# A fused attention, expert and gated-MLP kernel: the gate's tables behind group seven, one block of queries a group later, and unit 2's weights split in the units' loop

## The chip, the cores and the metric

The kernel runs on one core of a Trainium2 chip. The metric is the device time of one execution in microseconds (us); the time before is a median of three runs. The engines are named as the profile names them: PE (TensorE, matmuls; PEld its weight loads), DVE (VectorE), ACT (ScalarE), POOL (GpSimd) and SP (SyncE, which here only issues transfers).

## The reference

Three parts follow one another, on 2 x 768 tokens:

```python
# 1 attention, 2 batches x 8 heads, 768 tokens, head size 64
k_sum = k.reshape(B, H, nb, 32, D).max(axis=3)      # block maxima of the keys
v_sum = v.reshape(B, H, nb, 32, D).mean(axis=3)     # block means of the values
scores = [local scores (|i-j| < 16, else -1e9), scores with k_sum + log(32)]
a = softmax(scores); x = a @ [v, v_sum]             # then [1536, 512]
# 2 eight experts, each token goes to one
logits = x @ w_gate + modality_bias[modality_id]
e = argmax(logits); x = softmax(logits)[e] * (relu(x @ w1[e]) @ w2[e])
# 3 a dense layer 512 -> 2048 -> 512
h = x @ w_in; out = (h * tanh(softplus(h))) @ w_out
```

## The kernel before

**Attention.** It runs in 24 groups: 128 queries of one batch and of four heads each. A loop over steps g works on several groups at once: in step g it issues the scores of group g + 2 (`scores`), their row maxima on DVE (`top`, tile `nm`), the exponentials on ACT (`exps`, tile `a`), the reciprocal of their sums on DVE (tile `sm`) and the product of both (`normalize`, tile `an`, on DVE or POOL by the string `norm_by`), then the transposes of group g (`transpose_a`, `store_aT`) and the product with the values of group g - 1 (`values`, `store_xT`). All instructions of one engine run in the order in which this code issues them; semaphores order the engines among each other.

**What feeds the groups.** The tables `loads` and `prep`, by step, say when blocks of 256 queries or keys are loaded (SP) and prepared. A block is copied to `hp` (`pack`, one step ahead, engine by the fifth entry), transposed on PE, and written to SBUF: keys to `kt` (then, one step later, block maxima `ks` on DVE and windows `kw` on DVE or ACT), queries to `qb` in two halves (`q_chunk`, engines by the last entry: "VV" is both halves on DVE, "AV" the first on ACT, the second on DVE). A block is written ("q", batch, half of the heads, third of the tokens). POOL also adds up the values' block means (`vb`, `vm`), which come by transfer.

**The gate.** `small_loads` fetches three small inputs (`gm`, `mb`, `mi`) and `gate_tables` makes two tables of them on POOL: the identity beside the gate's weights in `gm`, which the first `gate_products` reads in step 10, and `bias_t`, which the first `choose` reads in step 12.

**Experts and dense layer.** Behind the groups stand 40 units of the experts' work (`step(u)`: `up_unit`, then `expert_down`, 24 and 12 matmuls on PE). Each needs its two weight tiles split into a high and a low part: `split_unit` issues one copy on ACT (`h`, L417) and one subtraction on DVE (`l`, L418) for each half. The table `hooks` starts this work inside the last groups: the splits of units 0, 1 and 2 in steps 22 and 24 and the first matmuls of unit 0 in step 25. In `step(u)` stands, for each unit, `split_unit(u + 1, 0)`, `split_unit(u, 1)`, `split_unit(u + 1, 1)`, `split_unit(u + 2, 0)`; a half that is split already is passed over. The accumulators of `expert_down` lie where the attention's PSUM tiles (`px` among them) lay. The dense layer is the last part.

Of the kernel before, what the change touches and what calls it, by code (L numbers as in the profile page):

```python
# [119 lines left out]
def attention_moe_mish_kernel(  # L120
# [17 lines left out]
    V, A, G, T = nc.vector, nc.scalar, nc.gpsimd, nc.tensor  # L138
# [282 lines left out]
    def load_w1(e, f, r1):  # L421
        nc.sync.dma_start(out=r1, in_=w1v[bass.ds(e, 1), :, :, f * 128:(f + 1) * 128].rearrange("o p k f -> p (o k) f"))

    def load_w2(e, f, r2):
        nc.sync.dma_start(out=r2, in_=w2v[bass.ds(e, 1), :, f, :].rearrange("o p d -> p (o d)"))
# [176 lines left out]
    def expert_reg(s):  # L602

        if s == 1:
            e_regs[1] = e_regs[0]
            return
        e = tab[0:1, 0, 0:1] if s == 3 else e_early[0:1, 0:1] if s == 0 else tab[0:1, 0, NSLOT:]
        e_regs[s] = reg(e, [ET.SP], E - 1)
# [9 lines left out]
    def load_first(n):  # L618

        for u in heads[:n + 1]:  # L620
            s, f = units[u]
            if (u, 0) not in asked and s in e_regs:
                asked.add((u, 0))
                raws[u, 0] = (extra if u == 3 else rw).tile([128, 4, 128], F32, tag="r1", name="r1")
                load_w1(e_regs[s], f, raws[u, 0])

    def load_second(u):
        if u >= len(units) or (u, 1) in asked or units[u][0] not in e_regs:
            return
        asked.add((u, 1))  # L630
        s, f = units[u]
        if s:
            raws[u, 1] = cout[:, NF2 // 2 + f, :].bitcast(F32)
        else:
            raws[u, 1] = extra.tile([128, DM], F32, tag="r2", name="r2", bufs=4)
        load_w2(e_regs[s], f, raws[u, 1])
# [377 lines left out]
    with ExitStack() as at:  # L1014
# [16 lines left out]
        raw, packed, kt, kw, ks, vw, vb, vm, qt = {}, {}, {}, {}, {}, {}, {}, {}, {}  # L1031
# [174 lines left out]
        def normalize(g, eng):  # L1206
            a, sm = st.pop(("a", g))
            an = thr.tile([128, 4, KC], F32, tag="an", name="an")
            eng.tensor_tensor(out=an, in0=a, in1=sm.unsqueeze(2).to_broadcast([128, 4, KC]), op=ALU.mult)
            st["an", g] = an  # L1210
# [177 lines left out]
        def gate_tables(mb, mi):  # L1388
            for j in range(4):
                G.tensor_scalar(out=gm[:, j, 0:128], in0=ident, scalar1=1.0, scalar2=0.0, op0=ALU.mult, op1=ALU.add)  # L1390
            mf = one.tile([128, 2, NT], F32, name="mf")
            mt = one.tile([128, 2, NT, E], F32, name="mt")
            for m in range(2):
                G.tensor_scalar(out=mf[:, m], in0=mi[:, :, 0], scalar1=float(m), scalar2=None, op0=ALU.is_equal)
                G.tensor_tensor(
                    out=mt[:, m], in0=mf[:, m].unsqueeze(2).to_broadcast([128, NT, E]),
                    in1=mb[:, m].unsqueeze(1).to_broadcast([128, NT, E]), op=ALU.mult,
                )
            G.tensor_tensor(out=bias_t, in0=mt[:, 0], in1=mt[:, 1], op=ALU.add)
# [48 lines left out]
            (22, 1): [("load",)],  # L1448
            (22, 2): [("split", 0), ("x", 1), ("x", 2), ("x", 3)],
            (24, 0): [("split", 1)],  # L1450
            (24, 2): [("split", 2)],
            (25, 0): [("up", 0)],
        }
        batches = [(0, 2), (2, 2), (4, 2), (6, 2), (8, 2)]
# [2 lines left out]
        def after(i, n):  # L1457
            return step_of[i] + n
# [88 lines left out]
        sums(1)  # L1547
        normalize(1, V)
        mb_mi = small_loads()
        gate_tables(*mb_mi)  # L1550

        def mixed(*parts):
            parts = list(parts)
# [7 lines left out]
        def mix(*parts):  # L1561
            for _ in mixed(*parts):
                pass
# [29 lines left out]
        def do_hook(x):  # L1593
            kind = x[0]
            if kind == "count":
                pc = pid[:, 448:448 + E]
                T.matmul(pc, cb[:, M_ONE:M_ONE + 128], ohsum)
                mix(choose_early(pc))
            elif kind == "load":
                expert_reg(0)  # L1600
                load_first(2)
                for u in range(3):
                    load_second(u)
            elif kind == "gather":
                V.tensor_copy(out=slot_ids, in_=pid[:, 0:E * NKP])
                of = small([128, NPIECE, E], "of")
                ids_ = pid[:, 0:E * NKP].rearrange("p (e k) -> p k e", e=E)[:, 0:NPIECE, :]
                V.tensor_tensor(out=of, in0=ids_, in1=early.unsqueeze(1).to_broadcast([128, NPIECE, E]), op=ALU.mult)
                fl = small([128, NPIECE], "fl")
                V.tensor_reduce(out=fl, in_=of, axis=AX.X, op=ALU.add)  # L1610
                V.tensor_copy(out=ids_early, in_=fl)
                xgs[0] = gather(None, new_rows())
                own()
                ids_reg(1)
            elif kind == "split":
                split_unit(x[1], 0)
                split_unit(x[1], 1)
                load_first(x[1] + 3)
                load_second(x[1] + 3)
            elif kind == "ids":  # L1620
                add_ids(*x[1:])
            elif kind == "x":
                some_x(0, x[1])
            elif kind == "up":
                up_unit(x[1])


        for g in range(NG + 2):
            if g == 16:
                first_p.close()  # L1630
                split_p = ctx.enter_context(tc.tile_pool(name="split", bufs=2, side="right"))
                cv = ctx.enter_context(tc.tile_pool(name="cv", bufs=1, side="right"))
                moe = ExitStack()
                late_moe = ExitStack()
                rw = ctx.enter_context(tc.tile_pool(name="rw", bufs=3, side="right"))
                hp = ctx.enter_context(tc.tile_pool(name="hp", bufs=2, side="right"))
                xp = ctx.enter_context(tc.tile_pool(name="xp", bufs=1, side="right"))
                extra = moe.enter_context(tc.tile_pool(name="extra", bufs=1, side="right"))
            for x in loads.get(g + 1, ()):
                do_load(x)  # L1640
            packs(g + 1)
            if g + 2 < NG:
                scores(g + 2)
                top(g + 2)
            for x in prep.get(g - 1, ()):
                if x[0] not in "qk":
                    do_prep(x)
            for i0, n in batches:
                if after(i0 + n - 1, 3) == g < NG and i0 != NEARLY:
                    add_ids(i0, n)  # L1650
            for x in hooks.get((g, 0), ()):
                do_hook(x)
            for x in prep.get(g, ()):
                if x[0] in "qk":
                    do_prep(x)
            if g < NG:
                if early_values[g]:
                    values(g - 1)
                transpose_a(g)
                if early_exps[g]:  # L1660
                    exps(g + 2)
                store_aT(g)
            if g + 2 < NG and not early_exps[g]:
                exps(g + 2)
            if g + 2 < NG - 1 or g == NG - 2:
                mix(place(g))
            for x in hooks.get((g, 1), ()):
                do_hook(x)
            if g + 2 < NG:
                sums(g + 2)  # L1670
                normalize(g + 2, V if norm_by[g + 2] == "V" else G)
            if g + 2 == NG - 1:
                mix(place(g))
            if 1 <= g <= NG:
                if g == NG or not early_values[g]:
                    values(g - 1)
                store_xT(g - 1)
            if g in gate_at:
                gate_products(gate_at[g])
                gate_store(gate_at[g])  # L1680
            for i0, n in batches:
                if step_of[i0 + n - 1] == g:
                    mix(choose(i0, n))
            if step_of[NT - 2] == g:
                mix(choose(NT - 2, 1))
            if step_of[NT - 2] + 1 == g:
                gate_exp(NT - 2, 1)
                mix(store_x(NT - 2, 1))
            if g in means_at:
                store_means(*means_at[g])  # L1690
            for x in hooks.get((g, 2), ()):
                do_hook(x)
# [122 lines left out]
```

## Time and profile before

| what | us |
|---|---|
| median of 3 runs (lowest, highest) | 572.18 (570.66, 573.83) |
| the profiled execution | 573.32 |
| its span | 571.3 |
| PE busy in the span | 533.4 |
| DVE, ACT, POOL busy | 390.7, 387.2, 95.5 |

The span is what the profile shows; 2.0 us lie around it. PE is busy for 93% of the span, but the first stages, up to some 140 us, are not bound by PE alone: there its waits are to be read one by one.

### The profile page before, as it was taken

Reading aid. Unit: us, or ns where it says so; the run is one execution under the profiler, and the core shown is the slowest. Engines: PE = TensorE matmul, PEld = TensorE weight load, DVE = VectorE, ACT = ScalarE, POOL = GpSimd, SP = SyncE. Lnnn points to the kernel's source line nnn. Section 1 sums busy time; section 2 is a strip of 40 time slices with the busy share of each in tenths; the row PEclk is TensorE's granted clock in tenths of the full one; section 3 lists DMA queues with packets and bytes.
Section 4 is the critical chain, followed back from the end, with each engine's and each line's share of the span. In section 5 each row is a group of like instructions: output and inputs, shape, how many; then the busy total and the mean of one; then the engine's idle time right before and its main releaser. Section 6 shows DMA issues by size and latency. Waiting matters only on the chain.

```text
span 571.3 us, 9001 instructions
## 1 busy us (share of the span) xinstructions
PE 533.4 (93%) x3086; PEld 462.7 (81%) x3086; DVE 390.7 (68%) x905; ACT 387.2 (68%) x793; POOL 95.5 (17%) x138
## 2 busy tenths in 40 slices
PE   4868799978999999999999999999999999999995
PEld 3857798868979998899988888888888888888883
DVE  3686889877777767688879998645664466456442
ACT  4756867566554535465578999778877887887771
POOL 5485542240604100000000000004000002100003
PEclk9998899989999999999999999999999999999999
DMA  8999961265754967634332331001000000100001
GB/s 210 176 226 205 181 107 37 75 170 183 242 178 142 335 198 244 211 121 129 111 112 80 104 107 41 1 1 73 1 0 1 0 2 37 38 0 1 0 1 73
DMA packets 75888, 59.34 MB, mean 104 GB/s; under 512 B 28838, under 2 KB 66214, under 8 KB 75456
## 3 DMA queue, kind: packets, MB, share of 16 engines
q1 hardware_dynamic: 73200, 52.36, 34.3%
q0 software_dynamic: 2640, 6.38, 3.2%
q8 instruction: 25, 0.41, 0.3%
q14 instruction: 23, 0.19, 0.1%
HBM read 51.25 MB, written 6.29 MB: 101 GB/s over the span
## 4 chain that ended last, share of the span: by engine, by line
PE 51%; DVE 2%; ACT 2%; issue 1%; POOL 0%; POOLq 0%; DVEq 0%
PE ph L539 22%; PE o L1719 22%; PE ph L467 4%; PE o L485 3%; ACT L577 0%; DVE l L418 0%; DVE cin L520 0%; DVE xg L580 0%; POOL out_dram L1736 0%; DVE mol L491 0%; ACT cin L516 0%; ACT xg L571 0%; ACT xg L577 0%; POOLq L1811 0%; DVE cin L519 0%
## 5 line engine op out<-in xcount | busy, mean ns | idle before, releaser
L580 DVE TENSOR_TENSOR xg<-xg,ph 128x512 f32<-128x512 f32 x48 | 30.8, 684 | 94.5 <-ACT xg L577 94.5
L571 ACT ACTIVATE xg<-ph,cf 128x512 f32<-128x512 f32 x48 | 33.0, 688 | 38.7 <-PE ph L539 38.0
L1736 POOL DMA_INDIRECT out_dram<-ot,rows x9 | 10.8, 1204 | 245.6 <-DVE xh L561 87.2
L467 PE MATMUL ph<-xh,h 128*128 128x290 f32 x160 | 50.2, 313 | 0.3 <-issue 0.3
L467 PE MATMUL ph<-xl,h 128*128 128x290 f32 x160 | 47.6, 297 | 0.4 <-DVE xl L451 0.4
L467 PE MATMUL ph<-xh,l 128*128 128x290 f32 x160 | 47.6, 298 | 0.3 <-DVE l L418 0.3
L1195 ACT ACTIVATE a<-ps,nm 128x120 f32<-128x120 f32 x96 | 33.4, 362 | 18.6 <-DVE nm L1187 12.1
L1181 PE MATMUL ps<-kw,qb 128*128 128x120 f32 x192 | 41.1, 342 | 5.1 <-DVE qb L1124 3.1
L1181 PEld LDWEIGHTS ps<-kw,qb 128*128 128x128 f32 x192 | 34.8, 227 | 7.7 <-ACT xT L1249 2.2
L539 PE MATMUL ph<-moh,l 128*128 128x512 f32 x96 | 38.0, 396 | 0.0
L1719 PE MATMUL o<-h,gl 128*128 128x512 f32 x96 | 37.9, 395 | 0.0
L1719 PE MATMUL o<-h,gh 128*128 128x512 f32 x96 | 37.9, 395 | 0.0
L1719 PE MATMUL o<-l,gh 128*128 128x512 f32 x96 | 37.9, 395 | 0.0
L539 PE MATMUL ph<-mol,h 128*128 128x512 f32 x96 | 37.9, 395 | 0.0
L539 PE MATMUL ph<-moh,h 128*128 128x512 f32 x96 | 37.9, 394 | 0.0
L417 ACT CAST h<-cout 128x512 fp32r<-128x512 f32 x32 | 19.8, 620 | 20.9 <-PE o L485 15.0
L539 PE MATMUL ph<-moh,xh 128*128 128x512 f32 x96 | 31.9, 393 | 0.0
L539 PE MATMUL ph<-moh,xl 128*128 128x512 f32 x96 | 31.9, 393 | 0.0
L467 PEld LDWEIGHTS ph<-xh,h 128*128 128x128 f32 x160 | 30.4, 190 | 1.4 <-issue 1.0
L467 PEld LDWEIGHTS ph<-xl,h 128*128 128x128 f32 x160 | 30.4, 190 | 1.3 <-issue 0.7
L572 ACT ACTIVATE xg<-xg 128x512 f32<-128x512 f32 x48 | 30.4, 632 | 1.5
L577 ACT ACT_TABLE_LOAD x24 | 30.8, 1283 | 0.4
(333 smaller groups left out, 1605.4 us busy)
## 6 DMA issues: line engine op xcount, KB each, us to landing
r<-in_moe_w_dram SPq DMA_DIRECT2D x32, 256.0 KB
cr<-in_moe_w_in_dram SPq DMA_DIRECT2D x16, 512.0 KB
cr<-in_moe_w_out_dram SPq DMA_DIRECT2D x16, 512.0 KB
cout<-in_moe_w_dram SPq DMA_DIRECT2D x16, 256.0 KB
cin<-in_moe_w_dram SPq DMA_DIRECT2D x16, 256.0 KB
k<-in_k_dram SPq DMA_DIRECT2D x12, 256.0 KB
q<-in_q_dram SPq DMA_DIRECT2D x12, 256.0 KB
vb<-in_v_dram SPq DMA_DIRECT2D x4, 768.0 KB
```

Source lines behind the costliest of these rows:

```text
L417: A.copy(out=h, in_=r)
L467: T.matmul(ph[:, :W], a[:, kk, :], b[:, kk, :], start=n == 0, stop=n == 11)
L485: T.matmul(po[d][:, :W], a[:, d * 128:(d + 1) * 128], b, start=f == 0 and n == 0, stop=f == F // 128 - 1 and n == 2)
L539: ins.append(T.matmul(pt, a[:, kk, :], b[:, kk, c0:c0 + 512], start=n == 0, stop=n == 11))
L571: A.activation(out=t, in_=hps, func=AF.Sigmoid, bias=cf[:, C_B0:C_B0 + 1])
L572: A.activation(out=t, in_=t, func=AF.Arctan)
L577: A.activation(out=t, in_=t, func=AF.Sin, scale=2.0)
L580: V.tensor_tensor(out=t, in0=t, in1=ph.pop(u), op=ALU.mult)
L1181: T.matmul(o, qc[:, j, t % 4, :], kw[b, hh][:, j, t, :], start=False, stop=True)
L1195: A.activation(out=a[:, j], in_=ps[:, j, 0:KC], func=AF.Exp, bias=nm[:, j:j + 1], accum_out=sm[:, j:j + 1],)
L1719: T.matmul(acc[m], a[:, m * 128:(m + 1) * 128], b, start=f == 0 and n == 0, stop=f == NF2 - 1 and n == 2)
L1736: ins = G.indirect_dma_start(out=out[:, :], out_offset=bass.IndirectOffsetOnAxis(ap=at_rows, axis=0), in_=ot[:, :], in_offset=None,)
```

## The change

The call of `gate_tables` moves from the place ahead of the loop to step 7 of the loop, behind that step's `normalize`. The block of queries ("q", 1, 1, 0) is prepared in step 10 instead of 9 (and so packed in step 9 instead of 8), and the first half of ("q", 1, 0, 0) is written by ACT instead of DVE. In step 24 unit 2 is no longer split; only the loads that came with it are issued there, and its two splits are issued by `step(0)` and `step(1)`.

```diff
-            9: [("kw", 1, 1, 1, "A"), ("kw", 1, 1, 2, "V"), ("k", 1, 1, 2, "G", "A"), ("q", 1, 0, 0, "G", "VV"), ("q", 1, 1, 0, "A", "VV")],
-            10: [("m2", 1, 1)],
+            9: [("kw", 1, 1, 1, "A"), ("kw", 1, 1, 2, "V"), ("k", 1, 1, 2, "G", "A"), ("q", 1, 0, 0, "G", "AV")],
+            10: [("q", 1, 1, 0, "A", "VV"), ("m2", 1, 1)],
...
-            (24, 2): [("split", 2)],
+            (24, 2): [("ahead", 5)],
...
         mb_mi = small_loads()
-        gate_tables(*mb_mi)
...
+            elif kind == "ahead":
+                load_first(x[1])
+                load_second(x[1])
...
                 normalize(g + 2, V if norm_by[g + 2] == "V" else G)
+            if g == 7:
+                gate_tables(*mb_mi)
```

On POOL the tables' six rows now stand behind the `normalize` of group 9 and ahead of the packing of the last block of keys and of the block of queries ("q", 1, 0, 0):

```order
 L1079 MEMSET kt 128x2x16
 L1209 TENSOR_TENSOR an<-a,sm 128x480
+L1390 TENSOR_SCALAR gm<-cf 128x128 x4
+L1394 TENSOR_SCALAR mf<-mi 128x12
+L1395 TENSOR_TENSOR mt<-mf,mb 128x96
+L1394 TENSOR_SCALAR mf<-mi 128x12
+L1395 TENSOR_TENSOR mt<-mf,mb 128x96
+L1399 TENSOR_TENSOR bias_t<-mt 128x96
 L1037 TENSOR_SCALAR hp<-k 128x512
 L1037 TENSOR_SCALAR hp<-q 128x512
```

The same six rows are gone from behind the first means (`vm`) and ahead of the `normalize` of group 2, where only two small memsets are left between the two.

On DVE, in steps 9 and 10, the rows of before read as follows (`qb_117` is the block ("q", 1, 0, 0), `qb_118` the block ("q", 1, 1, 0)):

```order
 L1187 TENSOR_REDUCE nm<-ps 128x4
 L1097 TENSOR_REDUCE ks<-kt 128x2x8 x2
-L1124 TENSOR_SCALAR qb_117<-ps 64x2x8x32 x2
-L1124 TENSOR_SCALAR qb_118<-ps 64x2x8x32 x2
+L1124 TENSOR_SCALAR qb_117<-ps 64x2x8x32
 L1203 TENSOR_SCALAR sm<-sm 128x4
 L1204 RECIPROCAL sm<-sm 128x4
```

Three of the four rows are gone there: one half of `qb_117` has moved to ACT, ahead of the exponentials of group 11, and DVE's own half waits for ACT's; the two of `qb_118` now stand one step later, behind the windows and ahead of the sums of group 12.

On ACT, where the units begin (`r_1712` and `r_1718` are unit 2's weight halves, `r_1735` one of unit 3's; `hh` is the hidden tile of units 0 and 1, `xr` copied from `px` frees the accumulators' place):

```order
 L1376 ACTIVATE xr<-xr,gs 128x512
+L473 ACTIVATE hh<-ph 128x290
+L1260 COPY xr<-px 128x512
 L417 CAST h<-r_1712 128x512
-L417 CAST h<-r_1718 128x512
-L473 ACTIVATE hh<-ph 128x290
-L1260 COPY xr<-px 128x512
 L1376 ACTIVATE xr<-xr,gs 128x512 x2
 L473 ACTIVATE hh<-ph 128x290
 L1289 ACTIVATE el<-lb 128x8
 L1376 ACTIVATE xr<-xr,gs 128x512
+L417 CAST h<-r_1718 128x512
```

Both casts stood ahead of the first `hh`; now one stands behind the copy of `px` and one behind the last scaling. DVE's two subtractions move in the same way. SP issues the same transfers in the same order as before.

## Rows read from the trace of the kernel before

**Rows 1.** Windows of the span: engines' busy time, PE clock, DMA share, GB/s

```profile
0.00:76.00 76.00, 56.57 (x379) 51.82 (x380) 53.83 (x100) 47.65 (x160) 44.76 (x69) 0.91 1.02 201
139.50:303.00 163.50, 160.75 (x1122) 149.02 (x1123) 124.72 (x318) 87.24 (x180) 18.93 (x28) 1.00 0.58 181
```

**Rows 2.** POOL's timeline, 18 to 37 us: start, duration, instruction, idle before and releaser

```profile
18.59 1.10 POOL L1390 TENSOR_SCALAR gm<-cf 128x128 f32<-128x128 f32 x4
27.50 0.26 POOL L1394 TENSOR_SCALAR mf<-mi 128x12 f32<-128x12 int32 x1 [7.81 <-DMA mi<-in_moe_modality_id_dram]
...
29.37 2.25 POOL L1209 TENSOR_TENSOR an<-a,sm 128x480 f32<-128x480 f32 x2
...
33.61 0.62 POOL L1037 TENSOR_SCALAR hp<-k 128x512 f32<-128x512 f32 x1 [1.20 <-DMA k<-in_k_dram]
34.20 2.35 POOL L1155 TENSOR_TENSOR vb<-vb 96x1024 f32<-96x1024 f32 x1
```

**Rows 3.** PE's timeline, 30 to 75 us, where it waited or a step begins

```profile
30.42 0.65 PE L1216 MATMUL pa<-cf,an 128*120 128x128 f32 x4 [1.78 <-POOL an L1209]
...
34.29 0.66 PE L1064 MATMUL px<-cf,hp 128*128 128x128 f32 x4 [0.58 <-POOL hp L1037]
...
38.37 0.45 PE L1181 MATMUL ps<-kw,qb 128*128 128x120 f32 x2 [2.04 <-DVE kw L1108]
...
68.57 0.74 PE L1181 MATMUL ps<-kw,qb 128*128 128x120 f32 x2
...
74.86 0.43 PE L1181 MATMUL ps<-kw,qb 128*128 128x120 f32 x2
```

**Rows 4.** DVE's timeline, 25 to 76 us

```profile
25.64 0.18 DVE L1204 RECIPROCAL sm<-sm 128x4 f32<-128x4 f32 x1
...
34.54 2.53 DVE L1103 COPY kw<-kt 128x960 f32<-128x960 f32 x1
...
49.71 2.75 DVE L1209 TENSOR_TENSOR an<-a,sm 128x480 f32<-128x480 f32 x1
...
62.88 2.32 DVE L1203 TENSOR_SCALAR sm<-sm 128x4 f32<-128x4 f32 x1
...
67.06 2.81 DVE L1124 TENSOR_SCALAR qb<-ps 64x512 f32<-64x512 f32 x4
...
72.98 0.65 DVE L1103 COPY kw<-kt 128x960 f32<-128x960 f32 x1
73.55 0.87 DVE L1108 COPY kw<-ks 128x576 f32<-128x576 f32 x1
74.35 1.23 DVE L1203 TENSOR_SCALAR sm<-sm 128x4 f32<-128x4 f32 x1
```

**Rows 5.** POOL's timeline, 49 to 75 us

```profile
49.58 5.39 POOL L1155 TENSOR_TENSOR vb<-vb 96x1024 f32<-96x1024 f32 x4 [3.37 <-DMA vb<-in_v_dram]
...
60.15 0.99 POOL L1209 TENSOR_TENSOR an<-a,sm 128x480 f32<-128x480 f32 x1 [2.10 <-ACT xT L1249]
61.10 0.96 POOL L1037 TENSOR_SCALAR hp<-k 128x512 f32<-128x512 f32 x1
...
62.61 2.56 POOL L1155 TENSOR_TENSOR vb<-vb 96x1024 f32<-96x1024 f32 x1
...
72.96 1.15 POOL L1037 TENSOR_SCALAR hp<-q 128x512 f32<-128x512 f32 x1 [1.46 <-DMA q<-in_q_dram]
```

**Rows 6.** Window of step 10, the same columns as rows 1

```profile
67.00:74.30 7.30, 5.80 (x28) 5.66 (x29) 6.23 (x12) 6.93 (x25) 2.33 (x3) 0.53 1.19 228
```

**Rows 7.** Timelines where the units begin: two rows of ACT, one of DVE, one of PE

```profile
136.48 1.12 ACT L417 CAST h<-r 128x512 fp32r<-128x512 f32 x2
...
138.92 0.59 ACT L1260 COPY xr<-px 128x512 f32<-128x512 f32 x1 [0.87 <-DVE lg L1258]
...
144.06 0.73 DVE L418 TENSOR_TENSOR l<-r,h 128x512 fp32r<-128x512 f32 x1 [0.95 <-ACT h L417]
...
139.55 0.40 PE L485 MATMUL o<-hh,h 128*128 128x290 f32 x1 [1.58 <-ACT xr L1260]
```

## The prediction
> **What bounds the kernel now.** I read the windows first. From 139.5 us on PE is busy 160.75 of 163.50 us: there only an earlier start helps. Up to 76 us PE is busy 56.57 of 76.00 and the transfers' share is 1.02 [rows 1], so two things bound this stage in turn: the arrival of blocks, and the chains of DVE, ACT and POOL between a block's arrival and PE's next scores. PE's timeline [rows 3] names the waits: 1.78 us for POOL's `an` of group 2, 0.58 for a block of keys, 2.04 for DVE's windows `kw`; and scores 12 begin only at 68.5 (row at 68.57). In POOL's timeline [rows 2] the reader sees why `an` was late: the tables waited 7.81 us for the transfer of `mi`, and `an` of groups 2 and 3 stood behind them until 29.37, though DVE had the reciprocal for group 2 at 25.8 [rows 4].
>
> One thing more is read from DVE against POOL. A copy of 128x960 took 2.53 us at 34.54 beside POOL's `vb` (34.20 to 36.55) and 0.65 at 72.98; an `an` took 2.75 at 49.71, where POOL's `vb` begins at 49.58; a `sm` of four columns took 2.32 at 62.88 and ended with POOL's `vb` of 62.61, at 65.2 [rows 2, 4, 5]. So a DVE instruction on SBUF that meets a POOL instruction waits for its end. `qb`, read from PSUM, kept 0.70 a piece.
>
> **The tables leave the early POOL.** `an` 2 then runs at 25.9 instead of 29.37 and `an` 3 at 28.5. PE's 1.78 goes, but its next matmuls need the block of keys that POOL packs at 33.61, and that waited 1.20 for its transfer [rows 2]; these stay at 34.29. At this point PE has won nothing. DVE and ACT have: exponentials and maxima of this step are 1.8 earlier, the copy of 34.54 begins at about 32.8, ahead of `vb`, and takes 0.65, and PE's 2.04 at 38.37 goes. The gain is 2.0 at scores 6.
>
> **What becomes of the 2.0.** POOL's `vb` at 49.58 was waiting for a transfer (3.37) [rows 5] and stays. `an` 7, 0.1 us late for it before, comes ahead of it with any gain over 0.2: 2.75 becomes about 0.7, another 2.1. Not all of it lasts. `an` 8 stands on POOL behind `vb` and its rest, so not ahead of 55.7, and the key block for step 8 arrives, as I estimate, at 53.5: `vb` landed at 49.5, and behind it lay another `vb` of 768 KB and this block of 256 KB, 5.2 us at the 201 GB/s of the window, partly moved already. From 53.5 the chain (two ACT copies, four exponentials, reciprocal, `an` 9) gives `an` 9 at 57.1 instead of 60.15: a gain of 3.05.
>
> **The tables' new place.** They cost POOL 1.10 for `gm` and 1.80 for the rest (27.50 to 29.3), 2.9 in all [rows 2], with no transfer left to wait for. POOL: `an` 9 to 58.1, tables to 61.0, the keys' pack 61.0 (61.10 before), the queries' pack to 62.3, then `vb` 62.3 to 64.9. So the tables eat the gain on POOL there, but push `vb` behind DVE's `sm` of group 10, which loses its stall of 2.1. DVE's two copies of windows and `sm` meet table instructions instead, for which I take 0.4 in all.
>
> Behind that wait stand, on POOL, these two packs, and PE's transposes for them (61.7 and 62.4). The chain for scores 12: DVE's `nm` 11 and two `ks` to 63.1, ACT's copies of blocks, windows and keys to 64.2, ACT's half of the queries to 64.8, then DVE's own half, 0.70, to 65.5. The change to "AV" takes 0.70 from DVE and adds 0.65 on ACT in series: I cost it at nothing. Scores 12 at 65.55 instead of 68.5: **2.95** ahead.
>
> **The block a step later.** In step 10 DVE now has both halves of it, 1.40 [rows 4], between windows and `sm` 12, and scores 13 wait for them: scores 12 (1.3 at 2.4 GHz, twice that at 1.2), `nm` 0.65, `ks` 1.27, windows 0.65, blocks 0.87, halves 1.40: 6.1, or 7.4 at 1.2 GHz. Before it was 74.86 - 68.5 = 6.35, bound by PE at a mean clock of 0.53 of full speed [rows 6]. So scores 13 are at 71.7 (3.2 ahead) or 72.9 (2.0 ahead). PE's four transposes, 0.6, lie under this. At the higher clock `sm` and `an` of group 12 then run ahead of POOL's pack at 72.96, which waits for a transfer and does not move [rows 5]; `sm` loses its stall of 1.1 (1.23 at 74.35) [rows 4]: up to 4.0 ahead. At the lower they meet it: 1.5 ahead.
>
> A rule of the Trainium skill speaks against this place: "SBUF — State Buffer", section "Who interferes with whom", has DVE's copies and two-input instructions and GpSimd exclude each other for a whole instruction. The trace agrees in the three rows above. By it each DVE instruction on SBUF that meets a table instruction pays up to that one's length, five at some 0.3 us, 1.5 instead of my 0.4, and the gain at scores 12 would be 1.9.
>
> **Unit 2's splits.** Before, ACT's two casts at 136.48 (1.12) stood ahead of unit 0's `hh` and of the copy of `px` at 138.92, for which PE's first `expert_down` waited 1.58, to 139.55 [rows 7]. Without them that copy ends at 138.15 and PE starts 1.4 earlier. But the casts come back: the second goes ahead of unit 3's, so ACT is 0.6 and DVE 0.7 later there, and the `l` that ended at 144.8 [rows 7] ends at about 145.1, where unit 3's matmuls (144.8 before) need it. PE, 1.4 ahead, waits for it. Sum -0.1; bounds +1.4 (if the cover of PE's queue is longer) and -0.5.
>
> **Sum.** 2.95 at scores 12, up to 4.0 two steps on, I take the middle, 3.5; less 0.1: 3.4. The steps from 13 to 24 wait for no transfer before or after, so the lead is handed on. The profiled execution took 573.32 (1.1 above the median, 572.18): 569.9, which is 568.8 on the median.
>
> **Rivals.**
> 1. PE's clock stays low in step 10. For it: by the chain above PE still waits for POOL's late packs and then for DVE's half ahead of scores 12, and in step 10 it was granted a mean of 0.53 [rows 6]. Against: these waits are shorter than before, since scores 12 come 2.95 earlier and the packs at most 0.5. Gain 1.5 - 0.1: 570.8. Chance 0.25.
> 2. The arrivals take nearly all. For it: PE's 34.29 stays, the window's share is 1.02, POOL waited, besides `mi`, three times for a transfer: 1.20, 3.37 and 1.46 [rows 2, 5]. Against: PE's 2.04 is DVE's. It decides if the copy now at 32.8 still falls behind `vb`. Gain 0.4: 571.8. Chance 0.13.
> 3. The tables become the new wait, and it is slower. Place: POOL ahead of the two packs of step 9. Without any gain before, `an` 9 ends at 61.1, tables at 64.0, the queries' pack at 65.3; scores 12 stay at 68.5 and step 10, at the lower clock, takes 7.4 instead of 6.35: +1.0, 573.2. It decides if `an` 9 ends later than about 60. Chance 0.07.
> 4. Unit 2's 1.4 is kept: 567.4. For it: PE was idle there; against: DVE's queue above. Chance 0.10.
>
> **The numbers.** The forecast (gain 2.9 to 4.0, 568.2 to 569.3) has 0.45. The bound for more than no change, 0.5%, is 2.9 us, 569.3. Faster: nearly all of the forecast and of rival 4, 0.53; same: rivals 1 and 2 and most of 3, 0.44; slower by 0.5% needs three times rival 3: 0.03. The range 567.0 to 571.8 leaves out rival 3 and the tails.
>
> **What would show it.** In the profile after: `an` of group 2 near 26 and no PE wait of 1.78; the wait of 2.04 gone; `an` 7 under 1 us; tables at about 58 to 61; scores 12 near 65.5; the first `expert_down` 1.4 closer to the transposes before it, with a new PE wait for `l` at unit 3. I am wrong if the copy at 32.8 or `an` 7 is still held up by `vb`, if scores 12 stand after 67, or if the low clock spreads over more of the steps than before.

## The result: slower by 0.5%, and the profile after

The changed kernel took 576.34 us (median of 20 runs, 569.15 to 579.73), the kernel before 572.36 (20 runs, 569.30 to 575.47). The ratio is 1.0054, with a 95% interval of 1.0027 to 1.0080. It leaves out the six of the 20 runs after that lie more than 1.5% above the fastest, the profiled one among them; the medians of all runs differ by 0.7%. The forecast was 568.8 and its range ended at 571.8: the sign was wrong. The profiled execution after took 578.88, 2.5 us above its median, so its rows show the order of the waits; sizes are taken from the experiments.

PE's timeline after, at the waits and at scores 10, 11, 12 and 13 (it answers to [rows 3]):

```profile
34.12 0.72 PE L1064 MATMUL px<-cf,hp 128*128 128x128 f32 x4 [3.19 <-POOL hp L1037]
...
55.98 2.36 PE L1237 MATMUL pv<-aT,vw 120*128 120x128 f32 x8 [4.58 <-DMA vw<-vm]
...
58.23 0.73 PE L1181 MATMUL ps<-kw,qb 128*128 128x120 f32 x2
...
63.08 0.43 PE L1181 MATMUL ps<-kw,qb 128*128 128x120 f32 x2
...
70.01 0.78 PE L1181 MATMUL ps<-kw,qb 128*128 128x120 f32 x2 [3.26 <-DVE qb L1124]
...
77.27 0.48 PE L1181 MATMUL ps<-kw,qb 128*128 128x120 f32 x2 [0.40 <-DVE qb L1124]
```

POOL's timeline after ([rows 2, 5]):

```profile
25.39 0.99 POOL L1209 TENSOR_TENSOR an<-a,sm 128x480 f32<-128x480 f32 x1 [6.40 <-DVE sm L1204]
...
33.45 0.62 POOL L1037 TENSOR_SCALAR hp<-k 128x512 f32<-128x512 f32 x1 [3.60 <-DMA k<-in_k_dram]
...
57.47 0.99 POOL L1209 TENSOR_TENSOR an<-a,sm 128x480 f32<-128x480 f32 x1 [1.52 <-DVE sm L1204]
58.42 1.09 POOL L1390 TENSOR_SCALAR gm<-cf 128x128 f32<-128x128 f32 x4
...
61.24 0.62 POOL L1037 TENSOR_SCALAR hp<-k 128x512 f32<-128x512 f32 x1
61.82 0.63 POOL L1037 TENSOR_SCALAR hp<-q 128x512 f32<-128x512 f32 x1
62.41 2.65 POOL L1155 TENSOR_TENSOR vb<-vb 96x1024 f32<-96x1024 f32 x1
```

DVE's timeline after ([rows 4]):

```profile
47.03 0.66 DVE L1209 TENSOR_TENSOR an<-a,sm 128x480 f32<-128x480 f32 x1
...
62.78 0.67 DVE L1097 TENSOR_REDUCE ks<-kt 128x16 f32<-128x512 f32 x1
63.37 2.02 DVE L1103 COPY kw<-kt 128x576 f32<-128x576 f32 x1
...
66.14 1.27 DVE L1097 TENSOR_REDUCE ks<-kt 128x16 f32<-128x512 f32 x2
69.26 0.70 DVE L1124 TENSOR_SCALAR qb<-ps 64x512 f32<-64x512 f32 x1 [1.85 <-ACT qb L1122]
```

Windows after, the columns as in [rows 1], two stretches in which PE ran at 1.2 GHz:

```profile
55.00:61.90 6.90, 5.92 (x26) 5.51 (x27) 1.37 (x4) 2.71 (x12) 5.14 (x15) 0.51 1.20 196
...
130.10:137.00 6.90, 6.90 (x32) 5.70 (x31) 3.60 (x8) 3.75 (x9) 0.00 (x0) 0.51 0.68 231
```

The queue of SP after, with the transfers that stand ahead of `vw<-vm`, and PE's row ahead of scores 12 in the kernel before, which [rows 3] leave out:

```profile
41.34 0.94 SPq L1141 DMA_DIRECT2D vb<-in_v_dram  x2
42.38 0.39 SPq L1042 DMA_DIRECT2D k<-in_k_dram  x1
42.86 5.08 SPq L1163 DMA_DIRECT2D vw<-vm  x4
```

```profile
68.50 0.28 PE L1180 MATMUL ps<-cb 67*128 67x120 bf16 x1 [3.04 <-DVE qb L1124]
```

The reader is to see three things. POOL did what was forecast, within half a us: `an` 2 at 25.39, `an` 9 at 57.47, tables from 58.42 to 61.3, the queries' pack done at 62.4. PE did not profit: it waited 4.58 us, until 55.98, for `vw<-vm`, the transfer of the block means of half 1 of batch 0, which the prediction had not looked at, and ran at half its clock behind it, 0.51 from 55.0 to 61.9 (scores 10 take 0.73 a pair, not the 0.43 of scores 11). And PE waits 3.26 us ahead of scores 12 for DVE's half of `qb`, which itself waited 1.85 us for ACT's. Before, PE waited 3.04 for `qb` at this place, so this wait is not new; it has a new reason (there DVE came late by `sm`'s stall [rows 4]).

### The profile page after: what moved, and what is told of

Read it like the earlier page. It is cut to its first block, busy times and chain, and to the rows that moved or that the text cites. A ratio compares the mean times of both kernels' runs of the same rounds, so it can differ in the third digit from the quotient of the medians.

```text
span 576.8 us, 8999 instructions
## 1 busy us (share of the span) xinstructions
PE 536.5 (93%) x3086; PEld 465.2 (81%) x3086; DVE 383.9 (67%) x904; ACT 388.0 (67%) x794; POOL 93.6 (16%) x138
## 4 chain that ended last, share of the span: by engine, by line
PE 50%; DVE 2%; ACT 2%; issue 1%; POOL 0%; POOLq 0%; DVEq 0%
PE ph L539 22%; PE o L1723 21%; PE ph L467 4%; PE o L485 3%; ACT L577 0%; DVE l L418 0%; DVE cin L520 0%; DVE xg L580 0%; POOL out_dram L1740 0%; DVE mol L491 0%; ACT cin L516 0%; ACT xg L577 0%; ACT xg L571 0%; POOLq L1815 0%; DVE cin L519 0%
## 5 line engine op out<-in xcount | busy, mean ns | idle before, releaser
L1237 PE MATMUL pv<-aT,vw 120*128 120x128 f32 x192 | 31.2, 313 | 6.2 <-DMA vw<-vm 4.6
L1237 PEld LDWEIGHTS pv<-aT,vw 120*128 120x128 f32 x192 | 27.6, 221 | 7.6 <-issue 5.0
```

What stands on the lines that cost most here:

```text
L1237: T.matmul(pv[:, 2 * j + n, :], w, aT[0:KC, 2 * j + n, :])
```

## The experiments

All twelve were timed in five rounds against the kernel before. "Ratio" is to that kernel, with its 95% interval. An interval is about 0.3% to either side, so a single one can't settle a part worth less; the profiles of the same runs show where PE waits. A profile is one execution: that of e9 is its fastest (570.63, median 575.09), that of e7 its slowest (576.39, median 572.10).

| run | what it has | ratio | interval |
|---|---|---|---|
| e1 | tables moved, alone | 0.9986 | 0.9958 to 1.0015 |
| e2 | queries' part, alone | 1.0051 | 1.0019 to 1.0082 |
| e3 | unit 2's splits, alone | 0.9966 | 0.9935 to 0.9996 |
| e6 | tables and unit 2 | 1.0007 | 0.9974 to 1.0041 |
| e9 | tables and queries | 1.0068 | 1.0043 to 1.0093 |
| e7 | half of (1,0,0) on ACT, alone | 1.0012 | 0.9978 to 1.0046 |
| e8 | (1,1,0) a step later, alone | 1.0033 | 1.0004 to 1.0063 |
| e5 | all of the change, means' transfers first | 1.0032 | 0.9998 to 1.0066 |
| e10 | as e6, means, then keys, then `vb` | 1.0020 | 0.9987 to 1.0054 |
| e11 | as e10, tables in the old place | 1.0042 | 1.0010 to 1.0074 |
| e12 | as e6, both `vb` last, summed later | 0.9990 | 0.9960 to 1.0020 |
| e13 | as e12, tables in the old place | 1.0015 | 0.9980 to 1.0049 |

**The three parts apart (e1, e2, e3).** My first theory, A, laid the loss on the wait for `vw<-vm` that the tables' move runs into; theory B on the queries.

```diff
 e1
-        gate_tables(*mb_mi)
+            if g == 7:
+                gate_tables(*mb_mi)
 e2
-  9: [..., ("q", 1, 0, 0, "G", "VV"), ("q", 1, 1, 0, "A", "VV")],
+  9: [..., ("q", 1, 0, 0, "G", "AV")],
+  10: [("q", 1, 1, 0, "A", "VV"), ("m2", 1, 1)],
 e3
-            (24, 2): [("split", 2)],
+            (24, 2): [("ahead", 5)],
```

Expected of e1: 

> Only the gate's tables are moved. Theory A (the lead made by the tables' move ends at one pin, PE's wait for the transfer of the block means of half 1 of batch 0, which lies behind two vb transfers; the idle time there lets TensorE's clock fall): the wait for vw<-vm of 3 to 5 us is there at about 56, the low clock follows it, scores 11 come at 62.5 to 63.5, and the time is 1.002 to 1.006 of before. Theory B (the loss comes from the block of queries a step later and ACT and DVE in series): scores 12 are 1.5 to 3 us ahead of the kernel before and the time is 0.994 to 0.998.

Expected of e2: 

> Only the block of queries a group later and the half on ACT. Theory A: the part costs nothing that can be measured, scores 12 within 0.7 us of before and scores 13 within 1, time 0.998 to 1.002. Theory B: scores 13 are 2 us or more later than before in the profile, time 1.003 to 1.007.

Expected of e3: 

> Only unit 2's splits in the units' loop. By the prediction's term (gain of up to 1.4 at the first expert_down, given back at unit 3's matmuls, where the weights are late): PE waits for h or l of unit 3 for some 0.8 us, the attention is as before, time 0.998 to 1.002. Rival C (the units' loop carries the loss): unit 3 starts 2 us or more later against the first expert matmuls than before, time 1.003 or more.

Theory A falls as the cause of the loss: the queries' part alone is 0.51% slower, the tables alone change nothing that can be measured (nor do they reach theory B's gain), and unit 2's part is, if anything, faster. PE's timeline in e3, whose attention is that of the kernel before, instruction for instruction:

```profile
54.27 1.19 PE L1237 MATMUL pv<-aT,vw 120*128 120x128 f32 x4 [3.06 <-DMA vw<-vm]
...
66.14 0.23 PE L1180 MATMUL ps<-cb 67*128 67x120 bf16 x1 [0.60 <-DVE qb L1124]
66.20 0.44 PE L1181 MATMUL ps<-kw,qb 128*128 128x120 f32 x2
...
70.93 0.48 PE L1181 MATMUL ps<-kw,qb 128*128 128x120 f32 x2
```

and in e1, with the tables moved:

```profile
53.62 0.68 PE L1237 MATMUL pv<-aT,vw 120*128 120x128 f32 x4 [3.77 <-DMA vw<-vm]
...
66.28 0.23 PE L1180 MATMUL ps<-cb 67*128 67x120 bf16 x1 [0.60 <-DVE qb L1124]
...
70.98 0.48 PE L1181 MATMUL ps<-kw,qb 128*128 128x120 f32 x2
```

From scores 12 on they agree within 0.15 us. So the wait for `vw<-vm` is there in the kernel before too, and what theory A said of the tables' lead is right as to where it goes, but wrong as to what it costs. In e3 scores 12 come at 66.2, not at 68.5 as in [rows 3]: the course on which the whole forecast was measured was not the only one (below). It also misled the expectation of e2: against that profile scores 13 of e2 are only 0.34 later, within theory A's 1 us, while the time is theory B's. So e2 is compared with e3. Now e2, the timelines of ACT, DVE and PE together:

```profile
65.58 0.61 ACT L1082 COPY kt<-pid 128x512 f32<-128x512 f32 x1
66.08 0.61 ACT L1122 ACTIVATE qb<-ps 64x512 f32<-64x512 f32 x1
...
66.72 0.70 DVE L1124 TENSOR_SCALAR qb<-ps 64x512 f32<-64x512 f32 x1 [1.86 <-ACT qb L1122]
67.47 0.50 PE L1181 MATMUL ps<-kw,qb 128*128 128x120 f32 x2 [2.23 <-DVE qb L1124]
...
72.32 1.52 DVE L1108 COPY kw<-ks 128x576 f32<-128x576 f32 x1
73.77 1.39 DVE L1124 TENSOR_SCALAR qb<-ps 64x512 f32<-64x512 f32 x2
...
75.20 0.48 PE L1181 MATMUL ps<-kw,qb 128*128 128x120 f32 x2 [1.87 <-DVE qb L1124]
```

Against e3, scores 12 are 1.27 later and scores 13 4.27. ACT's half stands behind the copies of windows and `kt` on ACT and starts at 66.08; DVE's half, free since 64.9, waits 1.86 for it. In step 10 both halves of the next block stand ahead of scores 13, where in e3 PE waited for nothing. In e3 unit 2's part does what the prediction said: PE's wait at the first `expert_down` is 0.76 (1.86 in e1) and it pays 0.50 for `h` and 0.34 for `l` at unit 3.

**The complements (e6, e9) and the halves of the queries' part (e7, e8).** e6 is the change without e2's lines, e9 without e3's; e7 has only `"VV"` to `"AV"` for (1,0,0), e8 only the move of (1,1,0) from 9 to 10.

Expected of e6: 

> The changed kernel with the queries' part undone: the tables behind group seven and unit 2's splits in the units' loop stay. Theory B (the queries' part carries the whole loss): scores 12 wait less than 1 us for qb, scores 13 none, time 0.993 to 0.999 of before. Theory D (the tables' move and the unit's splits each lose once they meet): 1.002 to 1.006.

Expected of e9: 

> The changed kernel with unit 2 split in step 24 as before: the tables' move and the queries' part together. Theory B: the same as the queries' part alone, 1.003 to 1.007, with PE's waits for qb ahead of scores 12 and 13, and no wait of PE for h or l of unit 3. Theory D: the two together lose more than the queries' part alone, 1.007 or more.

Expected of e7: 

> The kernel before with ACT writing the first half of the block (1,0,0); the block (1,1,0) stays in its step. Theory B1 (the half waits in ACT's queue behind four copies, and DVE's half behind it): DVE's own half starts after ACT's ends, near 66.5 where the rest of the course is like that of the run of the unit's part alone, scores 12 are 1 to 1.5 us later than in that run, PE waits 2 us or more for qb there, and scores 13 follow at the pace of before (4.7 us behind): time 1.001 to 1.003. If ACT and DVE in series cost nothing, as the prediction had it, scores 12 are within 0.3 of that run and the time is 0.999 to 1.001.

Expected of e8: 

> The kernel before with the block (1,1,0) prepared a step later; both halves of (1,0,0) stay on DVE. Theory B2 (two halves of 1.4 us ahead of scores 13, where PE had no wait before): PE waits for qb ahead of scores 13, scores 13 are 5.6 us or more behind scores 12 (4.7 in the run of the unit's part alone), scores 12 as there; time 1.002 to 1.005. If DVE has the room, scores 13 stay at 4.7 to 5.0 behind scores 12 and the time is 0.999 to 1.001.

Whatever stands beside it, the queries' part costs: e9 against e1 0.82%, the change against e6 0.47%, e2 alone 0.51%. The tables and the unit together, e6, are no change that can be measured, not the gain that theory B expected; theory D (tables and unit each lose once they meet something else) is not borne out: e6 lies below its range, though its interval reaches into it, and e9 stays just under it. Each difference of two ratios is known to some 0.4% only. PE in e9:

```profile
67.18 0.48 PE L1181 MATMUL ps<-kw,qb 128*128 128x120 f32 x2 [2.02 <-DVE qb L1124]
...
72.81 0.48 PE L1181 MATMUL ps<-kw,qb 128*128 128x120 f32 x2 [1.42 <-DVE qb L1124]
```

Here, at the full clock, scores 13 are 5.63 behind scores 12 (5.64 in e5, below, which has the same part); e1, e3 and e6 have 4.63, 4.73 and 4.65. e8 alone is slower by just more than its noise, e7 alone is not, though its PE waits 1.84 ahead of scores 12 and scores 12 are 1.74 later than in e3 (67.94); its scores 13 follow 5.84 behind, with scores 12 at 1.2 GHz, and not at the 4.7 expected. The two ratios add up to 1.0045, near e2's 1.0051.

In e6 scores 12 did not come early either: PE waited 1.58 for `qb`, until 68.23, where less than 1 was expected, though both halves are DVE's there. POOL's `vb`, pushed back by the tables, met DVE's copy of windows, which took 2.61 and not the 0.45 of e3 and e9:

```profile
62.17 2.36 POOL L1155 TENSOR_TENSOR vb<-vb 96x1024 f32<-96x1024 f32 x1
62.25 2.61 DVE L1103 COPY kw<-kt 128x576 f32<-128x576 f32 x1
```

So scores 12 of single profiles differ by a us or two for other reasons than the queries' part (67.18 in e9, with this part, 68.29 in e6, without it), and what "AV" costs is read within a profile (further down). DVE and PE in e8:

```profile
48.06 2.78 DVE L1209 TENSOR_TENSOR an<-a,sm 128x480 f32<-128x480 f32 x1
...
72.99 1.38 DVE L1124 TENSOR_SCALAR qb<-ps 64x512 f32<-64x512 f32 x2
...
74.45 0.45 PE L1181 MATMUL ps<-kw,qb 128*128 128x120 f32 x2
```

The halves end at 74.37, and scores 13 follow at 74.45, 7.26 behind scores 12. The wait for `qb` that I expected on PE is not there: at 1.2 GHz PE was busy until then. So this profile does not tell DVE's chain from the clock; e9's does.

**What the tables' lead runs into (e5, e10 to e13).** In e5 only the order of SP's transfers differs from the change:

```diff
-            5: [("vw", 0, 10), ("vb", 1, 0), ("vb", 1, 1), ("k", 1, 1, 1)],
+            5: [("vw", 0, 10)],
+            6: [("vb", 1, 0), ("vb", 1, 1), ("k", 1, 1, 1)],
```

Expected: 

> The changed kernel, with the transfers of vb(1,0), vb(1,1) and the keys (1,1,1) issued behind the four transfers of the means of half 1 instead of ahead of them. Theory A: PE's wait of 4.58 us for vw<-vm falls to under 2, the low clock of 55 to 62 goes or shifts, scores 10 come 2 us or more earlier than 58.23, and the time is 2 us or more below that of the changed kernel (ratio to before 0.996 to 1.001). If another arrival (the keys at 54.2, POOL's vb) pins the same stage, scores 10 move but scores 12 do not, and the ratio stays at 1.003 to 1.007. Theory B: no effect on the time, since the block of queries decides scores 12 and 13.

PE in e5, at scores 10 and at its next wait:

```profile
50.52 0.43 PE L1181 MATMUL ps<-kw,qb 128*128 128x120 f32 x2
...
55.52 0.67 PE L1064 MATMUL px<-cf,hp 128*128 128x128 f32 x4 [3.58 <-ACT kt L1082]
```

The wait for `vw<-vm` is gone and scores 10 come at 50.5 instead of 58.2. But PE stands 3.58 us a few matmuls on, for the keys (1,1,1), which ACT could pack only at 54.34, and the time, 1.0032, can't be told from the change's. The Trainium skill, "DMA: Bandwidth & Descriptors", section "Two DMAs through the same engine are not ordered", has the descriptors of one queue of a DMA engine start in order; the traces agree, since what is issued behind the two `vb` comes late, after the change the means, in e5 the keys. In e10 the keys go ahead of `vb` as well, `6: [("k", 1, 1, 1), ("vb", 1, 0), ("vb", 1, 1)]`, on e6; e11 is the same on e3.

Expected of e10: 

> The changed kernel without the queries' part, and SP issues the means of half 1 first, then the keys (1,1,1), then the two vb. Pin theory: PE's wait of 3.7 us for vw<-vm at 54 goes; the next pin is POOL, where the an of group 8 stands behind the vb that lands near 52, so its transposes come at 57 to 59 with a wait of 2 to 4 us on PE for POOL or an; scores 12 at 63 to 66 and the time 0.994 to 0.999 of before. If the arrivals did not hold the tables' gain back, nothing moves against the run without the queries' part: scores 12 at 66 to 68, time 0.999 to 1.002.

Expected of e11: 

> The same order of transfers, with the tables in their old place ahead of the loop (unit 2's splits in the units' loop, queries as before). If the tables' move is worth something once the pin is off, this is 0.002 to 0.005 slower than the run with the tables moved. If the tables behind group nine now hold up the packs of the keys and queries, it is the faster of the two by 0.002 or more. If the early 1.8 us of PE are absorbed by the next arrival in any case, the two agree within 0.002.

```profile
61.12 1.11 PE L1216 MATMUL pa<-cf,an 128*120 128x128 f32 x4 [7.61 <-POOL kt L1078]
```

PE in e10 now stands 7.61 us for POOL, where `an` of group 8 is behind the sums of the late `vb`: a larger wait than the one removed, and than the 2 to 4 expected. Scores 12 come at 69.20, not at 63 to 66, and the expected gain did not come. In e12 both `vb` go behind the keys and queries of step 7, and POOL adds them up in steps 9 and 11; e13 is e12 with the tables in their old place.

```diff
+            6: [("k", 1, 1, 1)],
-            7: [("k", 1, 1, 2), ("q", 1, 0, 0), ("q", 1, 1, 0), ("v", 1, 5)],
+            7: [("k", 1, 1, 2), ("q", 1, 0, 0), ("q", 1, 1, 0), ("vb", 1, 0), ("vb", 1, 1), ("v", 1, 5)],
...
-            5: [("m1", 1, 0), ("m2", 1, 0)],
-            7: [("k", 1, 0, 2, "A", "A"), ("m1", 1, 1), ...],
+            7: [("k", 1, 0, 2, "A", "A"), ...],
+            8: [..., ("m1", 1, 0), ("m2", 1, 0)],
+            10: [("m1", 1, 1), ("m2", 1, 1)],
...
-        means_at = {4: (0, 1), 8: (1, 0), 13: (1, 1)}
+        means_at = {4: (0, 1), 10: (1, 0), 13: (1, 1)}
```

Expected of e12: 

> As the run with the keys first, but the two vb are loaded behind the three blocks of keys and queries of step 7, and POOL adds them up in steps 9 and 11 instead of 6 and 8. Pin theory: no wait for vw<-vm, for kt or for the an of group 8 is over 1.5 us between 45 and 58; scores 10 before 54, scores 12 at 58 to 64; time 0.990 to 0.996 of before. If PE's low clock or a later arrival (queries of 69 to 74) takes the lead back, scores 12 are early but scores 16 are not (82 in the run of the unit's part alone) and the time is 0.998 to 1.002.

Expected of e13: 

> The same with the tables in their old place. With no pin behind it the late start of the an of groups 2 and 3 (the wait for mi) should be worth its 1.8 us of PE: scores 8 and 12 are 1 to 2.5 us later than in the run with the tables moved, and the time is 0.002 to 0.004 more. If they agree within 0.001, the tables' move is worth nothing even without the pin.

POOL and DVE in e12, in step 11:

```profile
69.95 5.33 POOL L1155 TENSOR_TENSOR vb<-vb 96x1024 f32<-96x1024 f32 x4
...
70.52 1.81 DVE L1203 TENSOR_SCALAR sm<-sm 128x4 f32<-128x4 f32 x1 [1.35 <-ACT a L1195]
...
72.58 1.58 DVE L1209 TENSOR_TENSOR an<-a,sm 128x480 f32<-128x480 f32 x1
```

No wait of PE over 0.4 us is left between 45 and 55, as expected; one of 2.30, for POOL's pack behind the tables, ends at 57.46, which was not. Scores 12 come at 61.94, 4.3 us before e3. Then POOL's later sums meet DVE's `sm` and `an` of group 13, 1.81 and 1.58 us instead of 0.17 and 0.66, and scores 16 are only 2.4 ahead (79.56). The time is the same as before. Between e10 and e11 and between e12 and e13 the ratios differ by 0.22% and 0.25%, less than the intervals, and the profiles don't bear out a gain of the tables' move: it leads by 1.8 and 2.8 at scores 10 (51.65 and 53.41, 50.66 and 53.47), but scores 12 come at 69.20 and 69.23, at 61.94 and 61.88, where 1 to 2.5 had been expected of e13. That the move gains once the way is free is not shown.

## Why the prediction was wrong

**The step that failed** is "The change to 'AV' takes 0.70 from DVE and adds 0.65 on ACT in series: I cost it at nothing", and with it "The block a step later", costed against a step of 6.35 us. Both mechanisms were named, both sizes of their chains were about right, and both were compared with the wrong thing. The gain that was to stand against them, 2.95 at scores 12, failed as well: by the reference, by the arrivals, and by "so the lead is handed on" (all below). The times show the cost of the two together, 0.5% (e2); how it is shared between them is read from profiles only.

- AV: by the prediction's own times DVE had the two `ks` done at 63.1, and with "VV" its two halves would have been written at 64.5; with "AV" it forecast 65.5. That 1.0 us was in the sum and was not seen as a cost, because the reference was 68.5. Measured: DVE, done with the two `ks`, waits for ACT's half 1.85 after, 1.86 in e2, 1.89 in e5, 1.85 in e7 and 2.46 in e9, in which it could have written the other half itself, 0.70; so "AV" costs 1.2 to 1.8 at scores 12. That is 0.2 to 0.3%, less than e7's interval can show.
- Step 10: the forecast chain is 6.1 at the full and 7.4 at the low clock. Measured: 5.63 in e9, 5.64 in e5 and 7.26 after (70.01 to 77.27). But the 6.35 of before belongs to a PE at 0.53 of its clock [rows 6]. At the full clock the kernel before takes 4.73 there (e3). So the move costs 0.9, and up to 3 where `vb` holds up DVE's copy (1.52 at 72.32 in e2) and the clock falls.

**The reference was one execution that ran late in the attention.** Five profiled executions, the kernel before's among them, have the same instructions of the attention up to 48 us. The clock of PE between 30 and 47 us and what `an` of group 7 took on DVE:

| execution | granted clock, 30 to 47 | `an` 7 at | took |
|---|---|---|---|
| before | 0.80 | 49.71 | 2.75 |
| e8 | 0.81 | 48.06 | 2.78 |
| e2 | 0.90 | 46.78 | 0.66 |
| e3 | 1.00 | 46.85 | 0.66 |
| e7 | 1.00 | 45.44 | 0.66 |

In the two with the lowest clock `an` 7 came after POOL's `vb` had begun and waited for its end; in the others it came first. That the clock decides it is likely, not shown. The 2.1 us that the tables' move was to win there, and `sm`'s stall of 2.1 at 62.88 [rows 4], which e3 does not have either (0.17 at 62.32), were mostly won already. e3 reached scores 14 4.66 us ahead of the profiled execution of before without any change to the attention.

**The lead is not handed on.** The sum has "The steps from 13 to 24 wait for no transfer before or after, so the lead is handed on". In the kernel before PE does wait for one there, `xg`, 2.40 us; e3 waits 2.33 and the kernel after 2.93. Before and e3, at this wait and in the window of 124 to 140 us, with the columns of [rows 1]:

```profile
126.64 0.25 PE L457 MATMUL ph<-cf,xg 34*128 34x34 f32 x1 [2.40 <-DMA xg<-xs,ids_early]
122.02 0.31 PE L457 MATMUL ph<-cf,xg 34*128 34x34 f32 x1 [2.33 <-DMA xg<-xs,ids_early]
...
124.00:140.00 16.00, 11.83 (x93) 10.48 (x91) 11.90 (x47) 10.45 (x26) 1.00 (x2) 1.00 0.71 215
124.00:140.00 16.00, 15.20 (x95) 13.60 (x94) 9.40 (x39) 8.54 (x20) 0.45 (x3) 0.76 0.42 136
```

In this window PE was granted the full clock in the one and a mean of 0.76 in the other. Of e3's lead of 4.4 us at scores 23, 1.5 is left at the first `expert_down` (138.01 against 139.55) and 0.3 in the time (573.02 against 573.32), though unit 2's part accounts for some of the last. From scores 23 to the first `expert_down` the profiles take 19.6 (e6) to 26.1 us (e7). So a lead or a loss at scores 12 is not one of the same size in the time.

**The tables.** Right: the early `an`, PE pinned at 34.29 (34.12 measured), the tables' place and price (2.9 forecast, 2.85), the packs unmoved, `an` 7 at 0.66. Scores 12 after 67, named as a sign of being wrong, came (70.01). Rival 2, the arrivals, was the case: it had 0.13, and I looked for it at the keys, not at `vw<-vm`, for which PE did not wait in the profile of before. The lead of the tables' move at scores 7 (3.0 us against the profiled execution of before, only 1.4 between e1 and e3) ends there. Rival 1, the low clock in step 10, came too (7.26, with 7.4 forecast), and one more stretch that it did not name: PE idles for `vw<-vm` and is granted 0.51 from 55.0 to 61.9. Rival 3 did not come: PE waits for `qb`, not for POOL's packs.

**DVE against POOL.** The stall of `sm` did go, but `vb` caught the `kw` copy in its place, 2.02 at 63.37 after and 2.61 in e6. In e3, without the tables in its way, `vb` ran at 58.17, ahead of these copies; the tables' new place pushes it among them. In e9, where the copy at 61.20 came ahead of `vb` at 63.02, it took 0.45. The tables themselves met no DVE copy: DVE stood idle from 57.3 to 60.88 for scores 10. So the 0.4 that I took and the 1.5 by the rule of the Trainium skill ("SBUF — State Buffer", section "Who interferes with whom") were both too much there; the rule itself agrees with the trace in e12's two rows. The prediction's own "a DVE instruction on SBUF that meets a POOL instruction waits for its end" is too wide: after, the reduction `ks` kept its 0.67 beside the `vb` of 62.41 that held up the `kw` copy. And `qb`'s 0.70 before met no POOL instruction (POOL stood idle from 66.57 to 70.51); it is e8's two halves at 72.99, 1.38 beside `vb`, that show it.

**Unit 2.** Right in the sum, -0.1, with both terms smaller than forecast (1.4 and 1.5). PE's timeline after, the first `expert_down` and unit 3:

```profile
143.81 0.40 PE L485 MATMUL o<-hh,h 128*128 128x290 f32 x1 [0.74 <-ACT xr L1260]
...
149.87 0.40 PE L467 MATMUL ph<-xh,h 128*128 128x290 f32 x1 [0.46 <-ACT h L417]
...
150.74 0.40 PE L467 MATMUL ph<-xh,l 128*128 128x290 f32 x1 [0.34 <-DVE l L418]
```

0.8 is won at the first (1.58 in [rows 7]) and 0.8 lost at unit 3.

**What stays open.** Each part's share is known to some 0.3% only: e1, e2 and e3 add up to 1.0003, and the whole was 1.0054. From e2, e9 against e1 and the change against e6 the queries' part is worth 0.6% on average, which is the whole loss; whether the tables or unit 2 add or take 0.1% is not settled. e3's 0.9966 did not come back in e6, so I don't call unit 2's part a gain. Nor do the times settle how the loss is shared between "AV" and the block a step later, and why the clock falls behind some of PE's waits and not behind others stays open.

## What to carry to other kernels

Measure a forecast against more than one execution of the kernel before: where a stall hangs on which of two instructions comes first, one profile shows one outcome, and gains counted on it may be there already. Follow a lead to the end of the program before it is counted as time. Giving half of a write to a second engine helps only if that engine's queue is shorter: read what stands ahead of the instruction on the new engine, and what the old one would have done meanwhile. When a lead is forecast, list every transfer that the next steps wait for, those too that show no wait now, because the first one that lands late ends it.

## What the runs showed of the hardware

The same instructions ran at a granted clock of 0.80 to 1.00 in the same stretch of five executions; e3's scores 23 (114.1) and those of the profiled execution before (118.6), behind the same instructions, are 4.4 us apart. Stretches at 1.2 GHz come behind PE's waits, but not the same ones each time: in e9 it is 1.2 GHz behind the wait at 54.11 and not behind those of 2.02 and 1.42 us. They also cost later: after, PE was busy all of 130.1 to 137.0 at 0.51 of its clock, behind a wait of 2.93 us for `xg`; behind a wait of 2.40 at the same place, before was granted 1.00. A DVE copy that met POOL's `vb` took 2.02 to 2.61 and not 0.45, a reduction beside it its usual 0.67. And four transfers of 72 KB, issued from 42.86 us on behind two of 768 KB and one of 256 KB, held PE until 55.98; issued ahead of these (e5), they held it no longer.
